# Longformer attention and a squared-ReLU MLP: full-width matmuls issued as two halves of 64 weight columns

## The chip, the cores and the metric

The kernel runs on one core of one Trainium2 chip. The metric is the time of one execution on the device in microseconds, the median of several runs. The profile shows TensorE's matmuls (PE), TensorE's weight loads (PEld), VectorE (DVE), ScalarE (ACT), GpSimd (POOL) and SyncE (SP), which here only issues transfers.

## The reference

Attention over 8 batches and 8 heads with 576 tokens of 64 elements. A token sees its neighbours within 32 positions, and 8 global tokens see all and are seen by all. The heads of a token are then put side by side (4,608 tokens of 512 elements) and go through an MLP.

```python
scores = scale * np.matmul(q, k.transpose(0, 1, 3, 2))
mask = np.abs(pos[:, None] - pos[None, :]) <= window
mask = mask | is_global[:, None] | is_global[None, :]
attn = softmax(np.where(mask, scores, -1e9))      # written out in the reference
x = np.matmul(attn, v) -> (batch * seq, heads * head_dim)
h = x @ w_in                                      # 512 -> 2048
g = np.maximum(h, 0.0) ** 2
out = g @ w_out                                   # 2048 -> 512
```

## The kernel before

All products are in fp16 with fp32 sums. Each matmul on TensorE is two instructions: a weight load, which puts the stationary operand into the array, and the matmul, which streams the moving operand past it. The profile writes the used part of the array as rows*columns, for example 128*128, 128*64 or 64*128, and the moving operand as partitions x columns.

**Attention** goes by units `i` of one batch and two heads, 32 in all, each in two halves of 288 tokens. For a half, `sc_mm` (L758) makes the transposed scores of both heads: 64 rows of the array for each head, so that two matmuls (64*128) share the array. ScalarE takes the exponential (`sc_exp`, L767), VectorE multiplies by the mask (`sc_mask`, L777). `pv_mm` (L799) then multiplies by the values and by a block of ones (which gives the sums): each has 64 weight columns, one head in the columns 0 to 63 and the other in 64 to 127, so that two matmuls (128*64) share the array. A half has 12 such matmuls, or 20 in the first batch's first halves. `pv_rec`, `pv_sum` and `pv_mul` (L809, L818, L840) divide and write `xT`; `scatter` (L861, GpSimd) puts in the rows of the global tokens.

**The MLP** goes by ten chunks of tokens, eight of 512 and two of 256. `mm1` (L526) makes blocks of `x @ w_in` with 128*128 weights and 512 or 256 moving columns; ScalarE takes the maximum with zero (L531), VectorE squares (L533). The first chunk's blocks are made by `mm1_half` (L556) in 256 columns, and its second product by `mm2` (L576) in 512. For the other chunks `mm2_fast` calls `product` (L639), which makes the second product from seven half-size products with 256 moving columns instead of eight; VectorE makes the sums of operands (L612, L618) and of results (L650, L653).

**Preparation.** The first two batches' q and k are transposed on TensorE (`transpose`, L480), with a one-hot product for the global tokens (L485, 8 moving columns). `mask_globals_matmul` (L353) and `values_sum` (L460) use the one-hot `oh` as weights, 8 columns wide. Later batches are transposed by DMA. `warm` (L293) issues matmuls on zeros while TensorE would be idle. `sc_mm` adds the mask by a matmul with the identity (L751) for the early units.

**Order.** The schedule is written out by hand; each engine takes its instructions in program order. MLP pieces wait in the list `fills`, and `fill(n)` takes pieces worth `n` from it between the steps of the attention. In the steady part, units 8 to 31, the order on TensorE is: scores of both halves, MLP pieces, PV of both halves, MLP pieces:

```python
        scores(i, 0)
        scores(i, 1)
        ...
        fill(4)
        ...
        pv_mm(i, 0)
        pv_mm(i, 1)
        ...
        fill(4)
```

So TensorE comes in and out of the scores once per unit, and in and out of the PV matmuls once per unit. After the last unit `take(len(fills))` makes what is left of the MLP.

Of the kernel before, what the change touches and what calls it, by code (L numbers as in the profile page):

```python
# [9 lines left out]
FP16 = mybir.dt.float16  # L10
# [8 lines left out]
NT = 5  # L19
# [3 lines left out]
TP = 96  # L23
# [27 lines left out]
def kernel(  # L51
# [10 lines left out]
    nc = tc.nc  # L62
    B, H, S, D = q.shape
    NG = global_idx.shape[0]
    dm = H * D
    dff = moe_w_in.shape[1]
    P = 128
# [14 lines left out]
    def sbt(name, shape, dtype, bufs=1, tag=None):  # L82
        return sb.tile(shape, dtype, name=name, tag=(tag or name), bufs=bufs)
# [12 lines left out]
    def pst(tag, shape, dtype=FP32):  # L96
        return psum["pool"].tile(shape, dtype, name=tag, tag=tag, bufs=psum["bufs"][tag])
# [12 lines left out]
    def token_rows(nm, i):  # L110
# [11 lines left out]
        for t in (  # L122
# [6 lines left out]
    vts = [  # L129
        early[:, 2 * NT * dm + VW * i : 2 * NT * dm + VW * (i + 1)].rearrange(  # L130
            "p (t e d) -> p t e d", t=NT, e=2
        )
        for i in range(2 * NHP)
    ]
# [88 lines left out]
    idle = sbt("idle", [P, 512], FP16)  # L223
# [18 lines left out]
    for base, cu, cm in (  # L242
# [3 lines left out]
            out=ub[0], in_=ub[0], compare_op=ALU.is_ge, fill=0.0,  # L246
# [4 lines left out]
    for col, base, cm in ((slice(0, 2), -8, 1), (slice(1, 2), KN[-1] + 7, -1)):  # L251
        nc.gpsimd.affine_select(
            out=rows[:, col], in_=rows[:, col], compare_op=ALU.is_ge, fill=0.0,
# [3 lines left out]
        out=ub[1], in_=ub[0], compare_op=ALU.is_ge, fill=0.0,  # L257
# [9 lines left out]
        out=tok, in_=tok, compare_op=ALU.is_ge, fill=-1.0,  # L267
# [7 lines left out]
    identity = sbt("identity", [P, P], FP16)  # L275
# [12 lines left out]
        fetch_tokens(nc.gpsimd, "q", i)  # L288


    def warm(bank, n):
        for _ in range(n):
            nc.tensor.matmul(bank, idle[:, 0:P], idle, start=True, stop=True)  # L293

    def keep_warm(n):
        warm(pst("at", [P, 2, 512])[:, 0], n)

    gbf = sbt("gbf", [P, NG], FP32)
    oh = sbt("oh", [P, NT, NG], FP16)
    ohp = sbt("ohp", [P, TJ, NG], FP16)  # L300

    g16 = sbt("g16", [1, NG], FP16)
# [9 lines left out]
    def one_hots(gb):  # L312
        nc.vector.tensor_copy(out=gbf, in_=gb)
        nc.vector.tensor_tensor(
            out=oh, in0=gbf.unsqueeze(1).to_broadcast((P, NT, NG)),
            in1=tok.unsqueeze(2).to_broadcast((P, NT, NG)), op=ALU.is_equal,
        )
        nc.vector.tensor_tensor(
            out=ohp, in0=gbf.unsqueeze(1).to_broadcast((P, TJ, NG)),
            in1=tokp.unsqueeze(2).to_broadcast((P, TJ, NG)), op=ALU.is_equal,  # L320
        )
# [23 lines left out]
    def mask_globals_matmul():  # L345


        mg = pst("at", [P, 2, 512])
        for half in range(2):
            wins = [x for x in WIN[half] if x[3] > 8]  # L350
            for i, (t, so, c0, w) in enumerate(wins):
                o = c0 - half * BANKC
                nc.tensor.matmul(  # L353
                    mg[0:NG, half, o : o + w], oh[:, t, :],
                    mask[:, MB[half] + so : MB[half] + so + w],
                    start=(i == 0), stop=(i == len(wins) - 1), skip_group_check=True,
                )
        return mg
# [96 lines left out]
    gls = {}  # L455

    def values_sum(i):
        gls[i] = pst("mm", [P, 512])[0:NG, 0 : 2 * D]
        for t in range(NT):
            nc.tensor.matmul(  # L460
                gls[i], oh[:, t, :], vts[i][:, t], start=(t == 0), stop=(t == NT - 1)
            )

    def values_place(i, op):
# [9 lines left out]
    def transpose(nm, i, idles=0):  # L474

        nat = nats[(nm, i)]
        tr = pst("mm", [P, 1024], FP16)
        warm(tr.bitcast(FP32), idles)
        for j in range(TJ):
            nc.tensor.transpose(  # L480
                tr[:, TP * j : TP * j + TP], nat[:, j, :], identity[0:TP, 0:TP]
            )
        gl = tr.bitcast(FP32)[:, 384 : 384 + NG]
        for j in range(TJ):
            nc.tensor.matmul(  # L485
                gl, nat[:, j, :], ohp[0:TP, j, :], start=(j == 0), stop=(j == TJ - 1),
                skip_group_check=True,
            )
        trs[(nm, i)] = tr[:, 0:S].rearrange("p (j q) -> p q j", j=TJ), gl
# [28 lines left out]
    def mm1(c, x):  # L518
        t0, T = CHUNKS[c]
        if c not in gts:  # L520
            gts[c] = sbt("gt", [P, NFF, TC], FP16)
        us = (x, x + NFF // 2) if T < TC else (x // 2 + x % 2 * (NFF // 2),)
        ph = pst("mm", [P, 512]).rearrange("p (j x) -> p j x", x=T)
        for j, u in enumerate(us):
            for t in range(NDM):
                nc.tensor.matmul(  # L526
                    ph[:, j], w_in[:, t, u * P : (u + 1) * P], xT[:, t, t0 : t0 + T],
                    start=(t == 0 and j == 0), stop=(t == NDM - 1), skip_group_check=True,
                )
        rl = sbt("rl", [P, TC], FP16, bufs=5).rearrange("p (j x) -> p j x", x=T)  # L530
        nc.scalar.activation(out=rl, in_=ph, func=AF.Relu)  # L531
        gt = gts[c].rearrange("p (j f) x -> p f j x", j=2)[:, x] if T < TC else gts[c][:, us[0] : us[0] + 1]
        nc.vector.tensor_tensor(out=gt[:, :, 0:T], in0=rl, in1=rl, op=ALU.mult)  # L533
        for p, lo, hi in sums_at(c, x):
            g_sum(c, p, lo, hi)
# [11 lines left out]
    def mm1_half(u, half, tiles=range(NDM)):  # L547

        if 0 not in gts:
            gts[0] = sbt("gt", [P, NFF, TC], FP16)  # L550
        if 0 in tiles:
            ph_now[u] = pst("mm", [P, 2, 256])
        ph = ph_now[u]
        for j in range(2):
            for t in tiles:
                nc.tensor.matmul(  # L556
                    ph[:, j], w_in[:, t, (u + j) * P : (u + j + 1) * P],
                    (xT if half else xA)[:, t, half * 256 : half * 256 + 256],
                    start=(t == 0 and j == 0), stop=(t == NDM - 1), skip_group_check=True,
                )  # L560
        if NDM - 1 not in tiles:
            return
        rl = sbt("rl", [P, TC], FP16, bufs=5).rearrange("p (j x) -> p j x", j=2)
        nc.scalar.activation(out=rl, in_=ph, func=AF.Relu)
        nc.vector.tensor_tensor(
            out=gts[0][:, u : u + 2, half * 256 : half * 256 + 256], in0=rl, in1=rl, op=ALU.mult
        )
# [3 lines left out]
    def mm2(c, m, part):  # L571
        if part == 0:
            po_now[m] = pst("mm", [P, 512])
        po = po_now[m]
        for f in range(part * 4, part * 4 + 4):
            nc.tensor.matmul(  # L576
                po, gts[c][:, f, m * P : (m + 1) * P], w_out[:, f, :],
                start=(f == 0), stop=(f == NFF - 1),
            )
        if part == 3:  # L580
            ot = sbt("ot", [P, dm], FP32, bufs=3)
            nc.vector.tensor_copy(out=ot, in_=po)  # L582
            r0 = CHUNKS[c][0] + m * P
            nc.sync.dma_start(out=out[r0 : r0 + P, :], in_=ot)
# [37 lines left out]
    def product(c, p, bank, s, first=True):  # L622
        if bank not in banks:
            banks[bank] = pst("mm", [P, 2, MH])
        for f in range(FH):
            if p in gsums:
                g = gsums[p][:, f, s * P : (s + 1) * P]
            elif p == 3:
                g = gts[c][:, f, s * P : (s + 1) * P]
            else:  # L630
                r0 = CHUNKS[c][1] // 2 + s * P
                g = gts[c][:, FH + f, r0 : r0 + P]
            if p in wsum:
                w = wsum[p][:, f]
            elif p == 2:
                w = w_out[:, f, 0:MH]
            else:
                w = w_out[:, FH + f, MH:dm]
            nc.tensor.matmul(  # L639
                banks[bank][:, s], g, w, start=(first and f == 0 and s == 0), stop=(f == FH - 1),  # L640
                skip_group_check=True,
            )
# [100 lines left out]
    def sc_mm(i, half, idles=0):  # L743

        kt, qt = kts[i % NBUF], qts[i % NBUF]
        win, W = windows(i, half)
        sc = scs[(i, half)] = pst("at", [P, 2, 512])
        warm(sc[:, 0], idles)
        if added(i, half):
            for e in range(2):  # L750
                nc.tensor.matmul(  # L751
                    sc[:, e, 0:W], identity, far[:, MB[half] : MB[half] + W],
                    start=True, stop=False, skip_group_check=True,
                )
        for t, so, c0, w in win:
            for e in range(2):
                r = slice(64 * e, 64 * e + 64)
                nc.tensor.matmul(  # L758
                    sc[:, e, so : so + w], kt[r, t, :], qt[r, c0 : c0 + w],
                    start=not added(i, half), stop=True, skip_group_check=True,  # L760
                )
# [355 lines left out]
```

## Time and profile before

| | us |
|---|---|
| median of 5 runs | 334.19 (331.57 to 335.84) |
| the profiled execution | 334.61 |
| its span, first to last instruction | 332.9 |
| TensorE matmuls, busy | 316.4 (95%), 3,121 instructions |
| TensorE weight loads, busy | 209.8 (63%), 3,121 instructions |
| VectorE, busy | 244.8 (74%) |
| ScalarE, busy | 202.7 (61%) |
| GpSimd, busy | 127.4 (38%) |

The mean granted clock of TensorE over the span is 0.989: 1.00 but for two stretches of 3.4 us before 36 us, and the last 1 us. A group line gives line, engine, operation, tiles written and read, shape and count; then the busy time of all of them together in us, with overlaps counted once, the mean duration of one in ns, and the engine's idle time just before them with what ended it. Matmuls overlap, so that mean x count is more than the busy time, and the distance between starts is the better measure of what one costs. In the timeline the first column is the start, the second the time from the first start to the last end of the instructions merged in that line.

### The profile page before, as it was taken

Reading aid. Unit: us, or ns where it says so; the run is one execution under the profiler, and the core shown is the slowest. Engines: PE = TensorE matmul, PEld = TensorE weight load, DVE = VectorE, ACT = ScalarE, POOL = GpSimd, SP = SyncE. Lnnn points to the kernel's source line nnn. Section 1 sums busy time; section 2 is a strip of 40 time slices with the busy share of each in tenths; the row PEclk is TensorE's granted clock in tenths of the full one; section 3 lists DMA queues with packets and bytes.
Section 4 is the critical chain, followed back from the end, with each engine's and each line's share of the span. In section 5 each row is a group of like instructions: output and inputs, shape, how many; then the busy total and the mean of one; then the engine's idle time right before and its main releaser. Section 6 shows DMA issues by size and latency. Waiting matters only on the chain.

```text
span 332.9 us, 8222 instructions
## 1 busy us (share of the span) xinstructions
PE 316.4 (95%) x3121; PEld 209.8 (63%) x3121; DVE 244.8 (74%) x600; ACT 202.7 (61%) x380; POOL 127.4 (38%) x222
## 2 busy tenths in 40 slices
PE   7857899999999999999999899999999999999995
PEld 3545677544467647754788645874587458747884
DVE  6746379648997788677867769876987698758465
ACT  3665548654865686668557288658765876363150
POOL 8555786528901960189000962039302000100000
PEclk9997899999999999999999999999999999999999
DMA  8999999999992999399915599369987400200211
GB/s 186 164 186 205 178 193 166 154 109 154 169 121 67 162 178 108 78 175 144 131 66 106 51 175 153 32 143 164 143 64 134 116 2 14 83 32 2 78 50 63
DMA packets 149906, 39.11 MB, mean 117 GB/s; under 512 B 133124, under 2 KB 149300, under 8 KB 149868
## 3 DMA queue, kind: packets, MB, share of 16 engines
q0 software_dynamic: 95408, 16.78, 65.7%
q1 hardware_dynamic: 54042, 21.23, 33.9%
q10 hardware_dynamic: 418, 0.59, 0.7%
q8 instruction: 24, 0.39, 0.5%
q14 instruction: 14, 0.11, 0.1%
HBM read 37.86 MB, written 17.29 MB: 166 GB/s over the span
## 4 chain that ended last, share of the span: by engine, by line
PE 57%; issue 18%; DVE 8%; ACT 5%; POOL 1%; POOLq 0%; DVEq 0%
PE mm L526 23%; PE mm L639 19%; PE at L799 5%; PE mm L556 3%; PE mm L576 3%; PE at L758 3%; ACT er L767 2%; DVE gt L533 2%; DVE mix L618 2%; DVE early L612 1%; DVE xT L840 1%; POOL xT L861 1%; PE mm L480 1%; DVE ot L582 1%; ACT rec L810 1%
## 5 line engine op out<-in xcount | busy, mean ns | idle before, releaser
L526 PE MATMUL mm<-xT,w_in 128*128 128x512 f16 (+1 forms) x576 | 114.3, 356 | 0.1
L531 ACT ACTIVATE rl<-mm 128x512 f16<-128x512 f32 x128 | 75.8, 599 | 36.7 <-PE mm L526 33.5
L526 PEld LDWEIGHTS <-w_in 128*128 128x128 f16 x576 | 55.1, 98 | 52.4 <-issue 0.3
L861 POOL COPY xT<-gx 128x4 f16 x64 | 17.6, 274 | 138.2 <-DVE xT L840 134.8
L533 DVE TENSOR_TENSOR gt<-rl 128x512 f16<-128x512 f16 x128 | 53.2, 423 | 22.5 <-ACT rl L531 20.7
L639 PEld LDWEIGHTS <-mix 128*128 128x128 f16 x640 | 60.7, 98 | 11.0 <-DVE mix L618 1.9
L767 ACT ACTIVATE er<-at 128x880 f16<-128x880 f32 x54 | 46.1, 904 | 15.3 <-PE at L758 15.3
L618 DVE TENSOR_TENSOR mix<-gt 128x1024 f16<-128x1024 f16 (+1 forms) x82 | 53.2, 673 | 0.2
L639 PE MATMUL mm<-early,mix 128*128 128x256 f16 x384 | 45.6, 273 | 1.2 <-DVE mix L618 1.2
L777 DVE TENSOR_TENSOR et<-er,mask 128x880 f16<-128x880 f16 x54 | 33.3, 617 | 17.5 <-ACT er L767 16.9
L809 ACT ACTIVATE rec<-at 128x288 f32<-128x288 f32 x64 | 25.8, 404 | 32.2 <-PE at L799 27.1
L840 DVE TENSOR_TENSOR xT<-at,rec 128x288 f16<-128x288 f32 x60 | 27.2, 453 | 9.7 <-ACT rec L810 9.0
L639 PE MATMUL mm<-early,gt 128*128 128x256 f16 x256 | 31.9, 273 | 0.7 <-DVE gt L533 0.4
L639 PE MATMUL mm<-w_out,mix 128*128 128x256 f16 x256 | 30.6, 273 | 0.0
L799 PE MATMUL at<-et,onesb 128*64 128x192 f16 (+5 forms) x400 | 30.3, 228 | 0.0
L810 ACT ACTIVATE rec<-rec 128x288 f32<-128x288 f32 x64 | 28.4, 443 | 2.0
L653 DVE TENSOR_TENSOR ot<-mm,pt 128x512 f32<-128x512 f32 (+1 forms) x36 | 22.7, 632 | 8.0 <-ACT pt L678 6.8
L639 PEld LDWEIGHTS <-gt 128*128 128x128 f16 x256 | 23.9, 98 | 6.9 <-DVE gt L533 2.0
L178 POOL DMA_DIRECT2D kscr<-in_k_dram x30 | 26.2, 1065 | 2.4 <-DMA w_out<-in_moe_w_out_dram 2.1
L185 POOL DMA_DIRECT2D qscr<-in_q_dram x24 | 23.8, 1400 | 0.6 <-DMA gscr_k<-gstk 0.6
L799 PEld LDWEIGHTS <-onesb 128*64 128x64 f16 x400 | 22.2, 113 | 0.0
L678 ACT COPY pt<-mm 128x512 f32<-128x512 f32 (+1 forms) x18 | 9.7, 539 | 20.4 <-PE mm L639 20.4
(121 smaller groups left out, 348.6 us busy)
## 6 DMA issues: line engine op xcount, KB each, us to landing
out_dram<-ot SPq DMA_DIRECT2D x32, 256.0 KB
qscr<-in_q_dram POOLq DMA_DIRECT2D x24, 144.0 KB, 7.7
kscr<-in_k_dram POOLq DMA_DIRECT2D x24, 120.0 KB, 4.1
w_in<-in_moe_w_in_dram POOLq DMA_DIRECT2D x4, 512.0 KB, 7.1
w_out<-in_moe_w_out_dram POOLq DMA_DIRECT2D x4, 512.0 KB, 16.8
stf<-in_v_dram POOLq DMA_DIRECT2D x12, 120.0 KB, 6.0
s16b<-in_v_dram POOLq DMA_DIRECT2D x12, 120.0 KB, 8.3
early<-in_v_dram SPq DMA_DIRECT2D x20, 60.0 KB
```

Source lines behind the costliest of these rows:

```text
L178: nc.gpsimd.dma_start(out=kscr[b][r0 : r0 + KN[t]].rearrange("s (h d) -> s h d", d=D), in_=k[b, :, KT * t : KT * t + KN[t]].rearrange("h s ...
L526: nc.tensor.matmul(ph[:, j], w_in[:, t, u * P : (u + 1) * P], xT[:, t, t0 : t0 + T], start=(t == 0 and j == 0), stop=(t == NDM - 1), skip_ ...
L531: nc.scalar.activation(out=rl, in_=ph, func=AF.Relu)
L533: nc.vector.tensor_tensor(out=gt[:, :, 0:T], in0=rl, in1=rl, op=ALU.mult)
L618: nc.vector.tensor_tensor(out=gsums[p][:, lo:hi, 0:TH], in0=g[0], in1=g[1], op=op)
L639: nc.tensor.matmul(banks[bank][:, s], g, w, start=(first and f == 0 and s == 0), stop=(f == FH - 1), skip_group_check=True,)
L767: nc.scalar.activation(out=er[:, :, 0:W], in_=scs.pop((i, half))[:, :, 0:W], func=AF.Exp, bias=0.0, scale=scale)
L777: nc.vector.tensor_tensor(out=et[:, :, 0:W], in0=er[:, :, 0:W], in1=mask[:, MB[half] : MB[half] + W].unsqueeze(1).to_broadcast((P, 2, W)), ...
L799: nc.tensor.matmul(acc[D * e : D * e + D, x, o : o + w], onesb if x else vt[:, t, e], et[:, e, so : so + w], start=(n == 0), stop=(n == le ...
L809: nc.scalar.activation(out=rec, in_=av[:, 1, :, 0:GTOK], func=AF.Ln)
L810: nc.scalar.activation(out=rec, in_=rec, func=AF.Exp, scale=-1.0)
L840: nc.vector.tensor_tensor(out=(xT if x0 else xA)[:, hp, x0 : x0 + HS].rearrange("p (k x) -> p k x", k=2), in0=av[:, 0, :, 0:GTOK], in1=rec ...
```

## The change

Every matmul that used all 128 weight columns is issued as two: weight columns 0 to 63 to the output's partitions 0 to 63, then columns 64 to 127 to partitions 64 to 127, both with the same moving operand. A new helper `halves` does it for `warm`, the one-hot product in `transpose`, `mm1`, `mm1_half`, `mm2`, `product` and the identity product in `sc_mm`; the transposes proper get their own loop. The one-hot `oh` is widened from 8 to 64 columns, cleared once, so that its two users have 64 weight columns as well. The PV matmuls had 64 columns already and stay. The scores keep 64*128, and the one small product of `indices` keeps its shape. Sums, sizes of buffers, and the order of the pieces stay as they were.

```diff
+    def halves(to, weights, moving, **flags):
+        for r in (slice(0, P // 2), slice(P // 2, P)):
+            nc.tensor.matmul(to[r], weights[:, r], moving, **flags)
+
     def warm(bank, n):
         for _ in range(n):
-            nc.tensor.matmul(bank, idle[:, 0:P], idle, start=True, stop=True)
+            halves(bank, idle[:, 0:P], idle, start=True, stop=True)
...
-    oh = sbt("oh", [P, NT, NG], FP16)
+    oh = sbt("oh", [P, NT, D], FP16)
+    nc.vector.memset(oh, 0.0)
...
-            out=oh, in0=gbf.unsqueeze(1).to_broadcast((P, NT, NG)),
+            out=oh[:, :, 0:NG], in0=gbf.unsqueeze(1).to_broadcast((P, NT, NG)),
...
-                    mg[0:NG, half, o : o + w], oh[:, t, :],
+                    mg[0:D, half, o : o + w], oh[:, t, :],
...
-        gls[i] = pst("mm", [P, 512])[0:NG, 0 : 2 * D]
+        gl = pst("mm", [P, 512])[0:D, 0 : 2 * D]
+        gls[i] = gl[0:NG]
         for t in range(NT):
             nc.tensor.matmul(
-                gls[i], oh[:, t, :], vts[i][:, t], start=(t == 0), stop=(t == NT - 1)
+                gl, oh[:, t, :], vts[i][:, t], start=(t == 0), stop=(t == NT - 1)
             )
...
         for j in range(TJ):
-            nc.tensor.transpose(
-                tr[:, TP * j : TP * j + TP], nat[:, j, :], identity[0:TP, 0:TP]
-            )
+            for r in (slice(0, D), slice(D, P)):
+                nc.tensor.transpose(
+                    tr[r, TP * j : TP * j + TP], nat[:, j, r], identity[0:TP, 0:TP]
+                )
         gl = tr.bitcast(FP32)[:, 384 : 384 + NG]
         for j in range(TJ):
-            nc.tensor.matmul(
+            halves(
                 gl, nat[:, j, :], ohp[0:TP, j, :], start=(j == 0), stop=(j == TJ - 1),
...
             for t in range(NDM):
-                nc.tensor.matmul(
+                halves(
                     ph[:, j], w_in[:, t, u * P : (u + 1) * P], xT[:, t, t0 : t0 + T],
...
         for f in range(part * 4, part * 4 + 4):
-            nc.tensor.matmul(
+            halves(
                 po, gts[c][:, f, m * P : (m + 1) * P], w_out[:, f, :],
...
-            nc.tensor.matmul(
+            halves(
                 banks[bank][:, s], g, w, start=(first and f == 0 and s == 0), stop=(f == FH - 1),
...
             for e in range(2):
-                nc.tensor.matmul(
+                halves(
                     sc[:, e, 0:W], identity, far[:, MB[half] : MB[half] + W],
```

The same replacement in `mm1_half` is left out here.

More of the change, by code (lines that the diff above doesn't have):

```diff
@@ L750, in sc_mm @@
             for e in range(2):
-                nc.tensor.matmul(
+                halves(
                     sc[:, e, 0:W], identity, far[:, MB[half] : MB[half] + W],
```

## The prediction

> **What bounds the kernel now.** I began with the busy table and the slices, then the chain of work that ended last, then the costliest groups, and last the timeline of TensorE.
>
> ```profile
> PE 316.4 (95%) x3121; PEld 209.8 (63%) x3121; DVE 244.8 (74%) x600; ACT 202.7 (61%) x380; POOL 127.4 (38%) x222
> ...
> PE 57%; issue 18%; DVE 8%; ACT 5%; POOL 1%; POOLq 0%; DVEq 0%
> ...
> L526 PE MATMUL mm<-xT,w_in 128*128 128x512 f16 (+1 forms) x576 | 114.3, 356 | 0.1
> ...
> L639 PE MATMUL mm<-early,mix 128*128 128x256 f16 x384 | 45.6, 273 | 1.2 <-DVE mix L618 1.2
> ```
>
> TensorE is busy 95% of the span, and its matmuls lead the chain. The two MLP lines waited 0.1 us and 1.2 us. By stretches PE is busy 30.4 of the first 40 us, 66.3 of 40 to 107, 190.9 of 107 to 300, and 28.7 of the last 32.9. So from 40 to 300 us time on TensorE is time of the kernel; before 40 us PE often waits for others, and after 300 us no attention is left.
>
> A busy PE can still lose time between matmuls. The timeline of TensorE shows it (start, duration, line, tiles, array rows*columns, shape, count):
>
> ```profile
> 221.65 2.46 PE L639 MATMUL mm<-early,mix 128*128 128x256 f16 x21
> 224.03 0.26 PE L799 MATMUL at<-et,stf 128*64 128x160 f16 x2
> 224.13 0.23 PE L799 MATMUL at<-et,onesb 128*64 128x160 f16 x2
> 224.20 0.25 PE L799 MATMUL at<-et,stf 128*64 128x192 f16 x2
> 224.28 0.25 PE L799 MATMUL at<-et,onesb 128*64 128x192 f16 x2
> 224.36 0.21 PE L799 MATMUL at<-et,stf 128*64 128x88 f16 x2
> 224.40 0.21 PE L799 MATMUL at<-et,onesb 128*64 128x88 f16 x2
> 224.44 0.22 PE L799 MATMUL at<-et,stf 128*64 128x112 f16 x2
> ...
> 224.76 0.23 PE L799 MATMUL at<-et,onesb 128*64 128x136 f16 x2
> 224.92 3.41 PE L526 MATMUL mm<-xT,w_in 128*128 128x512 f16 x15
> ```
>
> The 21 full-width matmuls of 256 columns last 2.46 us, one of them 0.273 us, so they start every (2.46-0.273)/20 = 109 ns. Those of 512 start every (3.41-0.38)/14 = 216 ns. The difference gives 0.418 ns per moving column and some 2 ns beside it. The last of the first group started at 221.65+2.46-0.273 = 223.84 and had streamed by 223.94; the first PV matmul starts at 224.03, about 95 ns later. The last PV pair, at 224.76, had streamed its 136 columns by 224.82; the next full-width matmul starts at 224.92, some 100 ns later. Neither gap has a releaser: it is the price of changing the way the array is divided. Scores (64*128) pay the same, 98 ns in and 95 ns out.
>
> **Part 1, the gaps that go.** I went through the matmuls in order of their starts. Full width and 128*64 are neighbours at 66 places, each some 97 ns (92 to 125, one of 244). From 40 to 300 us there are 60, together 5.87 us. After the change full width is 128*64, so these gaps shrink to the usual 2.5 ns: 5.87 - 60x0.0025 = 5.72 us. The second start after a change is late too: 94 ns after the first of 160 columns where 69 is usual (25 ns, some 28 times), 227 where 216 is usual (11 ns, some 32 times): 1.05 us more. Around the scores nothing goes: from 128*64 into the scores costs 98 ns and back 92, the few times that before has them, against 98 and 95 from full width. But coming out of the scores the second start is then late by 25 ns, not 11: 30 x 14 ns = 0.42 us to pay. Counted over the program, neighbours of different division fall from 154 to 80.
>
> **Part 2, a pair in the place of one matmul.** This is the dangerous part: 1,894 matmuls become pairs, 1,664 of them (576 of L526, 896 of L639, 128 of L556, 64 of L576) in the MLP. The PV rows above are such pairs: "x2" is two halves whose records start 2 to 4 ns apart. Pairs of 192 columns follow each other in 80 to 85 ns, of 88 in 40; over all PV the medians are 83, 60, 49.5 and 39 ns for 192, 136, 112 and 88 columns, where 0.418 ns per column and 2.5 would be 82.7, 59.3, 49.3 and 39.3. A pair therefore costs what one matmul does, to within some 0.35 ns. 1,664 x 0.35 = 0.6 us to pay. Below nothing I see no room: the columns must stream.
>
> [...] The rows:
>
> ```profile
> L526 PEld LDWEIGHTS <-w_in 128*128 128x128 f16 x576 | 55.1, 98 | 52.4 <-issue 0.3
> ...
> L799 PEld LDWEIGHTS <-onesb 128*64 128x64 f16 x400 | 22.2, 113 | 0.0
> ```
>
> A half load does last longer, 113 ns against 98. But 400 of them fill only 22.2 us, so they overlap, and pairs of 88 columns follow in 40 ns with two loads each. Loads of the two halves run beside each other and are no limit at 109 ns. [...]
>
> **Part 3, the small things.** In 16 transposes, 96 one-hot products of 8 columns go from 25 ns to the 30 ns of an 8-column PV pair; half of them lie after 40 us: 0.25 us. [...] Half rows in the accumulators change nothing for ScalarE and VectorE, which still wait for the second half. No DMA moves.
>
> **The sum.** 5.72 + 1.05 - 0.42 - 0.6 - 0.25 = 5.5 us on TensorE between 40 and 300 us. Beside gaps of this kind PE idles there some 7 us in spots where VectorE is later (0.5 us before the scores at 221 and 254 us, 1.2 us at 189); there a faster PE only waits longer, so I pass on 93%: 5.1 us. With the early 0.1 either way: 334.61 us of the profiled execution (span 332.9 and 1.7 around it) become 329.5. That execution stands 0.4 above the median of 334.19, so the median forecast is 329.1.
>
> **Rival 1: it does what it says and the gain is lost on the way.** A pair that costs 2 ns more than one matmul takes 3.3 us back, and VectorE (148 of 193 us busy from 107 to 300) or the half-speed clock that the early waits bring (0.50 granted in two stretches of 3.4 us, at 24.9 and 31.7) another 1 us: 333 to 334. For it: no pair longer than 192 columns is in the trace, and in none do both halves read the same moving data, as all will. Against: the four widths lie on one line. Chance 0.18.
>
> **Rival 2, on the other side: the front end.** PE's instructions grow from 6,244 to 10,032 in the program. A 256-column step, today two instructions in 109 ns, becomes four: 27 ns each. [...] The PV burst (48 instructions in 0.75 us) doesn't refute it, since the engine's queue could have been filled ahead. What speaks against it is PE's own semaphore steps, seen for the PV line while PE was still in the MLP:
>
> ```profile
> L799 PEldq EVENT_SEMAPHORE  x3: 51/51/51, 190.1 to 190.3; - x3
> ```
>
> They stand 125 ns apart, and the program has 8 instructions (4 MATMULs) between one and the next; less the 51 ns step that is 9 ns each, 31 ns a MATMUL at most with everything counted. Where the queue was full (222.0 to 222.9) the same steps stand 436 ns apart, the pace of the array. Instruction fetch grows from 24 to some 40 blocks of 16 KB, each 0.9 to 2.0 us and needed every 7 us. Chance 0.10, and 0.05 for a pair that costs over 5 ns more for another reason (both halves on the same addresses): 338 to 342.
>
> **How the numbers follow.** Forecast 0.67, 329.1 with 326.5 to 331.5 (pair cost 0 to 1 ns, share passed on 0.8 to 1.1, the early clock 1.5 us either way). Rival 1, 331.5 to 336. Slower cases 0.15, from 337 up. About 0.04 lie under 326.5 and 0.15 above 336, so the range is 326.5 to 336. One per cent is what a measurement can tell from no change (330.9 and 337.5 are its ends): faster 0.67, same 0.19, slower 0.14.
>
> **What would show it.** Right: in the timeline of after, a 256-column pair every 109 to 110 ns and a 512-column pair every 216; the PV pair following the MLP pair with no 95 ns; 98 and 92 ns still at the scores. Wrong: pairs at 113 ns and more, or pairs whose second half starts a full stream after the first; "issue" gaps between pairs in long MLP runs; a granted clock under 1.00 after 40 us.

## The result, and the profile after

The changed kernel takes 332.23 us (median of 42 runs, 329.68 to 336.46) against 333.46 us (79 runs): a ratio of 0.9971, 95% interval 0.9957 to 0.9984. By that ratio it is 1.0 us faster where 5.1 us were forecast. The ratio, here and below, is that of the runs in the faster of each kernel's two states, so it isn't quite that of the medians. The time lies in the range; the gain is a fifth of the one predicted. The profiled execution of the changed kernel took 335.48 us (span 333.7), 3.2 us above its own median, so the two profiled totals are not compared below; stretches of the two traces are.

The page of the changed kernel: its busy table, its instruction queue (transfers, MB) and its costliest groups (busy us, mean ns | idle before):

```profile
PE 313.3 (94%) x5015; PEld 239.5 (72%) x5015; DVE 244.9 (73%) x601; ACT 202.1 (61%) x380; POOL 127.3 (38%) x222
...
q8 instruction: 39, 0.64, 0.8%
...
L293 PE MATMUL mm<-xT,w_in 128*64 128x512 f16 (+1 forms) x1280 | 124.0, 350 | 2.3 <-DVE ot L589 2.0
L293 PEld LDWEIGHTS <-w_in 128*64 128x64 f16 x1408 | 80.8, 110 | 46.8 <-issue 6.7
...
L293 PE MATMUL mm<-early,mix 128*64 128x256 f16 x768 | 45.8, 273 | 1.2 <-DVE mix L625 1.2
```

All the full-width matmuls now stand at line 293, the helper. Twice the number of matmuls of 256 columns keep TensorE busy for 45.8 us, against 45.6 before: the pairs run side by side. A half load lasts 110 ns against 98, and it hides. What is new is at the end of the first L293 row: TensorE waited 2.0 us for `ot` of VectorE, which it did not do before. And the instruction queue brought 39 blocks of 16 KB in the place of 24 (`q8 instruction: 24, 0.39, 0.5%` on the page of before).

The timeline of TensorE in the changed kernel around a block of scores, where before had 95 to 100 ns on either side of the PV matmuls:

```profile
220.28 0.23 PE L806 MATMUL at<-et,s16b 128*64 128x136 f16 x2
220.34 0.23 PE L806 MATMUL at<-et,onesb 128*64 128x136 f16 x2
220.40 1.91 PE L293 MATMUL mm<-early,mix 128*64 128x256 f16 x32
222.25 0.36 PE L765 MATMUL at<-qt,kt 64*128 64x160 f16 x6
223.07 0.37 PE L765 MATMUL at<-qt,kt 64*128 64x112 f16 x6 [0.46 <-DVE xT L847]
223.37 2.81 PE L293 MATMUL mm<-early,mix 128*64 128x256 f16 x48
```

The last PV pair starts at 220.34 and streams 136 columns, 0.06 us; the MLP starts at 220.40. That gap is gone. The 32 halves in 1.91 us are 16 pairs every (1.91 - 0.273)/15 = 109 ns. So the pairs cost what the forecast said, and the gaps go where it said. But two lines below stands the other half of the story: in the middle of the scores TensorE waits 0.46 us for VectorE, and that wait has grown. The same place in before:

```profile
221.01 0.37 PE L758 MATMUL at<-qt,kt 64*128 64x112 f16 x6 [0.35 <-DVE xT L840]
```

**The steady part, counted.** Between the same two score blocks (starts at 101.28 and 280.33 us before, 104.43 and 281.22 after) I took, for each matmul, its start less the end of the stream of the one before. Gaps of 60 to 140 ns, the price of a change of division, fell from 8.08 to 3.94 us: 4.1 us, as forecast for the 44 places there (4.2 us). Longer gaps, each of which VectorE ends, rose from 8 with 3.44 us to 13 with 5.47. The stretch itself went from 179.05 to 176.79 us: 2.3 us of 4.1, or 55%, came through. It isn't the noise of one profile: in all eleven traces with `mm1` and `product` halved this stretch takes 175.95 to 176.79 us, and in the five with both at full width 179.03 to 179.15; so 2.3 to 3.1 us of 4.2 come through. TensorE's waits from 100 to 285 us, before and then after (us in total, times, longest):

```profile
PE mm L639 <- DVE mix L618: 1.0, 1, 1.0
PE at L758 <- DVE xT L840: 0.7, 2, 0.3
```

```profile
PE mm L293 <- DVE gt L540: 1.1, 2, 0.7
PE mm L293 <- DVE mix L625: 1.0, 1, 1.0
PE at L765 <- DVE xT L847: 0.9, 2, 0.5
PE at L806 <- DVE et L784: 0.2, 1, 0.2
```

VectorE sets TensorE's start at more places, and at the old ones a little later.

**The early part, lost twice.** At 44 us the changed kernel's scores stood 1.8 us ahead of before's (42.63 against 44.45). At 61 us the lead was 0.2 us, at 83 us it had become a delay of 2.9 us (86.08 against 83.15). The first loss has no semaphore in it. Two parts of TensorE's timeline after, from 43 to 54 us:

```profile
43.84 0.33 PE L487 MATMUL mm<-identity,natk 96*64 96x96 f16 x4
44.46 0.32 PE L487 MATMUL mm<-identity,natk 96*64 96x96 f16 x5 [0.29 <-issue]
45.23 0.26 PE L487 MATMUL mm<-identity,natk 96*64 96x96 f16 x3 [0.45 <-issue]
...
52.13 0.17 PE L293 MATMUL mm<-ohp,natq 96*64 96x8 f16 x1
52.91 0.33 PE L293 MATMUL mm<-ohp,natq 96*64 96x8 f16 x11 [0.61 <-issue]
53.09 1.04 PE L293 MATMUL mm<-xT,w_in 128*64 128x256 f16 x16
```

Twelve transposes that belong together are torn into 4, 5 and 3; a group of twelve gathers into 1 and 11. "issue" says that the engine waited for nothing that the profile shows. The second loss has a releaser, here in the timelines of TensorE and of VectorE:

```profile
78.73 3.64 PE L293 MATMUL mm<-xT,w_in 128*64 128x512 f16 x32
84.39 1.76 PE L293 MATMUL mm<-xT,w_in 128*64 128x512 f16 x8 [2.01 <-DVE ot L589]
```

```profile
83.64 0.69 DVE L589 COPY ot<-mm 128x512 f32<-128x512 f32 x1 [2.84 <-DMA out_dram<-ot]
```

Before ran five accumulators through at the same place, with no wait:

```profile
78.73 4.48 PE L526 MATMUL mm<-xT,w_in 128*128 128x512 f16 x20
```

An accumulator here is a block of sums that takes one bank, a buffer of the pool `pst` in the memory called PSUM; eight half matmuls or four full ones fill it. In the changed kernel the fifth after the first chunk waits for its bank; the fourth output copy frees it; the copy needs one of three `ot` buffers, and waits 2.84 us until the first output has landed. TensorE stood still for 2.0 us, and its clock was granted at half for the next 3.4 us (from 84.6 us).

### The profile page after: what moved, and what is told of

Its sections match the earlier page's. It is cut to its first block, busy times and chain, and to the rows that moved or that the text cites. A ratio compares the mean times of both kernels' runs of the same rounds, so it can differ in the third digit from the quotient of the medians.

```text
span 333.7 us, 12010 instructions
## 1 busy us (share of the span) xinstructions
PE 313.3 (94%) x5015; PEld 239.5 (72%) x5015; DVE 244.9 (73%) x601; ACT 202.1 (61%) x380; POOL 127.3 (38%) x222
## 4 chain that ended last, share of the span: by engine, by line
issue 44%; POOL 21%; DMA 20%; PE 11%; POOLq 1%; DVE 1%; SPq 0%; ACT 0%
PE mm L293 11%; DMA qscr<-in_q_dram 5%; DMA w_out<-in_moe_w_out_dram 5%; POOL kscr L178 5%; DMA early<-in_v_dram 4%; POOL qscr L185 4%; POOL xT L868 4%; DMA qt<-qscr 3%; POOL s16b L207 2%; POOL stf L207 2%; DMA w_in<-in_moe_w_in_dram 2%; DMA stf<-in_v_dram 1%; POOL mix L868 1%; POOLq L868 1%; POOL s16b L152 1%
## 5 line engine op out<-in xcount | busy, mean ns | idle before, releaser
L293 PE MATMUL mm<-xT,w_in 128*64 128x512 f16 (+1 forms) x1280 | 124.0, 350 | 2.3 <-DVE ot L589 2.0
L293 PEld LDWEIGHTS <-w_in 128*64 128x64 f16 x1408 | 80.8, 110 | 46.8 <-issue 6.7
L538 ACT ACTIVATE rl<-mm 128x512 f16<-128x512 f32 x128 | 74.8, 599 | 39.9 <-PE mm L293 37.0
L293 PEld LDWEIGHTS <-mix 128*64 128x64 f16 x1280 | 68.5, 110 | 3.5 <-DVE mix L625 1.7
L293 PE MATMUL mm<-early,mix 128*64 128x256 f16 x768 | 45.8, 273 | 1.2 <-DVE mix L625 1.2
L816 ACT ACTIVATE rec<-at 128x288 f32<-128x288 f32 x64 | 25.8, 404 | 26.3 <-PE at L806 22.9
L293 PEld LDWEIGHTS <-gt 128*64 128x64 f16 x640 | 34.5, 110 | 8.7 <-DVE gt L540 2.4
L293 PE MATMUL mm<-early,gt 128*64 128x256 f16 x512 | 32.0, 273 | 1.5 <-DVE gt L540 1.4
L293 PE MATMUL mm<-w_out,mix 128*64 128x256 f16 x512 | 30.9, 273 | 0.0
L765 PEld LDWEIGHTS <-kt 64*128 64x128 f16 x400 | 12.6, 97 | 15.3 <-issue 13.6
```

Source lines behind the costliest of these rows:

```text
L293: nc.tensor.matmul(to[r], weights[:, r], moving, **flags)
```

## The experiments

Every ratio is to the kernel before, timed beside it. The theory at the start: the main part (mm1 and the weight product) gains, and something takes the gain away; the first question was where.

### Twice the same, and the two parts alone

> The kernel before, a second profile of it. Theory F (floor): until about 73 us the transfers and GpSimd set when unit 8 may start; the start of the MLP's main part does not depend on TensorE, so unit 8's scores start at 72 to 74 us again. Theory C (clock): half-width matmuls wake TensorE's clock later than full-width ones; then the clock of before reaches 1.00 at about 8 us again, as in its first profile (7.8 us).

> The changed kernel, a second profile of it. Theory F: unit 8's scores start at 72 to 74 us whatever the early clock does, and from there to the end each unit is 0.2 us shorter than before. [...]

Before again took 333.91 us, after again 333.99, one run each. Neither theory held. Unit 8's scores began at 72.2 and 73.3 us, as F had said, but at 69.4 in `e1_main` below, so there is no such floor; and C, by which the halved kernel gets its full clock late (16.3 us in its first profile), fell with the 6.9 us of `a2`. Single profiles of one kernel can stand 5 us apart at 30 us already: the seventh block of scores begins at 30.3 us in `a_bank` and at 25.1 in `a_again`, the same kernel further down. The early clock is granted differently in each, in full from 6.6 to 18.7 us on and then at half for stretches of 3.4 to 13.7 us. Both losses were there again in `a2`: three pauses (0.64, 0.51 and 0.77 us) from 44 to 55 us, and 1.63 us of waiting on `ot` at 84 us.

`e1_main` is before with halves in two places only; `e2_early` has them everywhere else:

```
-                nc.tensor.matmul(
+                halves(
                     ph[:, j], w_in[:, t, u * P : (u + 1) * P], xT[:, t, t0 : t0 + T],
...
-            nc.tensor.matmul(
+            halves(
                 banks[bank][:, s], g, w, start=(first and f == 0 and s == 0), stop=(f == FH - 1),
```

> Halves only in mm1 and product, the main part of the MLP; everything before and chunk 0's MLP stay full width. Theory F: the 0.2 us per unit of the steady part stays whole, so 3 to 4.5 us less than before and as fast as the changed kernel or up to 1.5 us faster: 329.5 to 332. Theory C: the gain that the changed kernel loses early comes back, 328.5 to 330. If the main part itself takes something back, 332.5 or more.

> The complement: halves in everything but mm1 and product. Theory F: no change within 0.7 us of before (332.8 to 334.2), since what is gained before 73 us waits for transfers. Theory C: slower than before by 1.5 to 3 us, 335 to 336.5. The sum of the changes of e1_main and e2_early should be the change of the whole, -1.2 us, within 1 us.

`e1_main` took 332.07 us, ratio 0.9976 (0.9952 to 0.9999); `e2_early` 335.55 us, 1.0058 (1.0030 to 1.0085). The early edits alone make the kernel slower; the time lies where C had put it, although C had fallen. The changes of the two parts, -0.8 and +1.9 us, do not add up to the whole, -1.0; they had been expected to, within 1 us. In both traces TensorE stood still near 80 us until the fourth output copy had ended (1.18 us, which the profile puts down to "issue" although the copy ended 0.06 us earlier, and 1.11 us), so that wait comes with either part, and neither part's halves can be its cause by themselves.

### The banks

In the compiled programs the `mm` accumulators are the same tiles in the same order in both kernels, but not in the same PSUM banks. Which bank is given out is decided when the program is built. From the fifth accumulator after the first chunk on, the plan of the changed kernel differs (bank 3 where that of before took bank 1); so does that of the 13 accumulators of the preparation, from the fourth on. I wrote the order of before into the changed kernel by hand, and the reverse:

```
+    BANK = {3: iter("0100100101010"), 2: iter("0321032103201320...")}
...
+        if tag == "mm":
+            tag = "mm" + next(BANK[psum["bufs"]["at"]])
+            return psum["pool"].tile(shape, dtype, name="mm", tag=tag, bufs=1)
```

> The changed kernel with each accumulator of the MLP placed by hand in the bank that it had in the kernel before. Theory B (bank): the wait of TensorE at about 84 us comes from the other bank, and goes: 1 to 2 us less than the changed kernel, 330 to 331.2, and no wait of over 0.3 us between unit 8's PV and unit 9's scores. Theory F (transfers set the floor): the wait only moves to the next scores, time as the changed kernel's, 331.8 to 332.8.

> The kernel before, full width, with the accumulators placed by hand in the banks that the changed kernel uses. Theory B: it gets the wait at about 80 to 84 us, 0.8 to 1.8 us slower than before: 333.8 to 335. Theory F: as before within 0.4 us.

> Halves in mm1 and product alone, with the banks of the kernel before. Theory B: the steady gain of 2.5 us or so comes through whole: 330 to 331. Theory F: as without the banks, about 332.

> Halves in everything but mm1 and product, with the banks of the kernel before. Theory B: of the 2 us that this kernel lost to the kernel before, 1 us comes back: 333.8 to 334.8; what is left (0.5 to 1.5 us) is the early part's own loss, in transposes and the clock. Theory F: 335.5 again. If the early part alone gains as its gaps promise, it is below 333.

The changed kernel with the banks of before took 331.76 us, ratio 0.9943 (0.9916 to 0.9969); before with the banks of the changed one 334.57 us, 1.0031 (1.0008 to 1.0055). `e1_bank`, `e1_main` with the banks of before, took 331.26 us, 0.9917 (0.9894 to 0.9941), and `e2_bank` 334.66 us, 1.0027 (1.0002 to 1.0051). All four move the same way, by 0.3 to 0.6%: 1.0 to 2.0 us for a choice that no line of the diff makes. The time of `a_bank` missed its forecast (330 to 331.2), and that of `e1_bank` missed by 0.3 us.

The traces are the firmer evidence. The thirteenth block of scores begins at 61 us in before and the seventeenth at 83. This stretch takes 21.4 to 22.2 us in all ten traces with the banks of before, and 22.9 to 25.2 in all six with those of the changed kernel, whatever is halved. And `b_bank`, full width everywhere, has the wait at the fifth accumulator:

```profile
77.62 3.62 PE L531 MATMUL mm<-xT,w_in 128*128 128x512 f16 x16
82.46 1.02 PE L531 MATMUL mm<-xT,w_in 128*128 128x512 f16 x4 [1.22 <-DVE ot L587]
```

With the banks of before it goes from this place, but where everything is halved a part comes back one accumulator later, just after the scores: 0.45 us in `a_bank`, 0.87 in `a_again`.

The main part's halves bring 2.8 us (0.9917), and the early edits still cost 0.9 us (1.0027) with the banks as they were.

### The pauses

Looked at instruction by instruction, TensorE stops in the early part before instructions that carry no wait. A pause is given here as the distance between two starts; the idle time in the rows is less. Counted from 0 over its weight loads, matmuls and semaphore instructions in order of their starts, it stopped before number 1729 in the changed kernel, in `a2`, `a_bank` and `e2_bank`, before 705 in the changed kernel and `a_bank`, and before 1985 in the changed kernel and `e2_bank`. These numbers are multiples of 256 apart, and the transfers of 16 KB on the instruction queue agree: the changed kernel has 3,788 loads and matmuls more and 15 such transfers more, 253 for each. I call the numbers the grid. At each of them the pause ended 2.2 to 2.5 us after such a transfer had started (for 1729 in the changed kernel: start 50.53, landed 51.41, next instruction 52.91). Before has no such pause between 40 and 62 us. From the eighth to the thirteenth block of scores (44 to 61 us in before) the four traces with everything halved take 18.0 to 18.4 us, the seven with `mm1_half` at full width 16.1 to 16.6.

The grid does not explain all of it. The transposes torn into 4, 5 and 3 above lie off it (numbers 1358 and 1368), and those two pauses, 0.49 and 0.64 us, are nearly half of the 2.4 us in that trace.

Three experiments: the transposes and their gathers alone back to full width (`e3_tr`, the other halves and the banks of before kept); the reverse, `e1_bank` with only these halved (`e4_dense`); and `e1_bank` with a run of small matmuls at its end, to see the supply by itself (`m_fetch`).

```
-            for r in (slice(0, D), slice(D, P)):
-                nc.tensor.transpose(
-                    tr[r, TP * j : TP * j + TP], nat[:, j, r], identity[0:TP, 0:TP]
-                )
+            nc.tensor.transpose(
+                tr[:, TP * j : TP * j + TP], nat[:, j, :], identity[0:TP, 0:TP]
+            )
...
-            halves(
+            nc.tensor.matmul(
                 gl, nat[:, j, :], ohp[0:TP, j, :], start=(j == 0), stop=(j == TJ - 1),
```

```
     take(len(fills))
+    tail = pst("at", [P, 2, 512])[:, 0, 0:8]
+    for _ in range(400):
+        nc.tensor.matmul(tail, idle[:, 0:P], idle[:, 0:8], start=True, stop=True)
+    for _ in range(400):
+        halves(tail, idle[:, 0:P], idle[:, 0:8], start=True, stop=True)
```

> The changed kernel with the accumulator banks of before, and only the transposes with their gathers (48 instructions a pair of tiles) put back to full width. Instruction supply theory: the early part loses because the halved transposes use up instructions at 90 in a us, and TensorE then pauses with no semaphore wait (0.6 to 1.1 us each, at instruction 1344, 1729 and 1985 of TensorE in the profiles) until the next 16 KB of its program is there. At full width the pauses go (about 2.0 us), and eight changes of width near four groups of transposes come back (8 x 97 ns = 0.8 us): 1.2 us less than with the halves, ratio about 0.991, no pause over 0.4 us without a wait between 40 and 62 us. Rival, that the early part loses to the clock or to the first transfers: the pauses stay or move, only the changes of width are added, ratio about 0.997.

> The kernel with halves in mm1 and the product alone and the banks of before (ratio 0.9917), and the transposes with their gathers halved as well; mm1_half and mm2 stay full. Supply theory: pauses without a wait come into the early part, where the transposes follow full-width matmuls at 18 instructions in a us, so fewer than in the changed kernel: 0.5 to 1.5 us, and eight changes of width add 0.8 us; ratio 0.996 to 0.999. Rival (clock or transfers): no pauses, 0.8 us of changes alone, ratio 0.994.

> The best kernel so far, with 400 full-width matmuls of 8 columns and then 400 pairs of halves of 8 columns at its end, which nothing waits for; they are extra work and no part of the computation. Supply theory: 800 instructions at 80 in a us (10 us) meet three pauses of about 1 us, 1600 at 130 in a us (12 us) meet six of about 1.5 us, one in every 256 instructions, each ending about 2.4 us after the start of a 16 KB instruction transfer; the whole about 34 us, though the transfers of data are over by then. Rival (pauses come from full data queues only, or from the first part alone): no pauses, 22 us.

`e3_tr` took 329.04 us, 0.9866 (0.9817 to 0.9915), and no pause was left between 40 and 62 us. `e4_dense` took 329.50 us, 0.9904 (0.9869 to 0.9939), against 0.9917 for `e1_bank`: halving the transposes cost nothing there, and its trace has no pause either. I had expected 0.5 to 1.5 us of pauses; with 0.9904 both theories missed (0.996 to 0.999, and 0.994). One measure accounts for both runs: the time from the start of a transfer to the first instruction of the block that it brings (on the grid: 1217, 1473, 1729, 1985). For transfers between 40 and 62 us it is 6.7 and 10.4 us in before, 5.4 and 6.7 in `e3_tr` and 3.2 and 3.7 in `e4_dense`. Wherever TensorE paused on the grid it is 2.2 to 2.5 us, and in no trace is it anywhere shorter than 2.2. The transfers of this part start some 75 to 265 instructions ahead of their block. With everything halved, the two transposes of a pair of tiles and their gathers are 96 instructions in some 0.9 us, and `mm1_half` four in 109 ns: a hundred instructions can pass in 1.0 us. Full-width transposes are 48 in the same 0.9 us, and halved ones beside a full-width `mm1_half` (two in 109 ns) are followed by a slower stretch. In both the block is there in time. What starts a transfer is not shown by the traces.

`m_fetch` took 361.02 us. Its tail lasted 33.2 us, near the 34 expected, but not for the reason given. The timeline of TensorE at its end:

```profile
348.29 3.58 PE L298 MATMUL at<-idle 128*64 128x8 f16 x128
352.02 6.13 PE L298 MATMUL at<-idle 128*64 128x8 f16 x213 [0.15 <-issue]
```

The whole groups between pauses are 128 matmuls, that is 256 instructions with their loads. The longest steps stand before numbers 10177, 10433, 10689, 10945, 11201 and 11457, each 256 after the last and on the same grid as 1729; they end 2.3 to 2.6 us after the start of a transfer, in the quiet end of the program. So the period and the delay were right, and full data queues are not needed for them. But the steps last 0.17 and 0.34 to 0.35 us, two of them only 0.07 where 0.05 is usual, not 1.5; and the full-width run had none (2.7 and 2.8 us from transfer to block): here the transfer began 145 to 210 instructions ahead, and 75 passed in a us, less than the 130 that I had put in. Most of the length of the tail goes with the clock, which was granted at half from 329.3 us to the end: the pairs of 8 columns stood 53 ns apart there, where the PV pairs of 8 columns took 30 at the full clock.

### Are the two losses separate?

`e5_tr_only` is the changed kernel with the same lines of `transpose` back to full width, and the scheduler's own choice of banks (that of the changed kernel from the fifth accumulator on).

> The changed kernel with only the transposes and their gathers put back to full width; the scheduler chooses the banks, and from the fifth accumulator after the first chunk on its choice is that of the changed kernel, not that of before. If the pauses of the instruction supply and the banks are two separate losses, this run keeps the second and is free of the first: the ratio of the changed kernel, 0.9971, less what the transposes brought with the banks of before (0.9943 to 0.9866, -0.0077): 0.989, no pause without a wait over 0.4 us between 40 and 62 us, and TensorE's wait of 1 to 2 us on VectorE near 80 us. Rival, that e3's gain was the clock or a lucky set of runs: 0.994 to 0.998, as with the halved transposes.

331.37 us, 0.9951 (0.9930 to 0.9973): the 0.989 of the theory is outside, and the rival's 0.994 to 0.998 came true, though not its reason, as the next pair shows. The pauses at 52 and 59 us were gone, but one of 0.52 us stayed at 44.8, and TensorE stood still for 1.32 us at 82 us until the output copy had ended. So with the banks of the changed kernel, full-width transposes bring 0.20% (0.9971 to 0.9951), where with those of before they had brought 0.77%. The pair was run once more side by side:

> The kernel of e3_tr once more (banks of before, transposes at full width, all else halved), now beside its pair with halved transposes on one chip. Width of the transposes and banks as two separate losses: full-width transposes bring what they brought with the changed kernel's banks, 0.9971 to 0.9951, so 0.9923 here against 0.9943. The one hiding the other (the wait of TensorE on VectorE near 80 us takes what the early part gains, and with the banks of before nothing takes it): 0.986 to 0.989, as in the five runs of e3_tr.

> The kernel of a_bank once more (banks of before, everything halved), as the other half of the pair: 0.9943 by its earlier runs, whichever holds; the difference to e3_again is the price of halving the transposes where the wait near 80 us is out of the way: 0.2% if the losses are separate, 0.5 to 0.8% if that wait hid it.

`e3_again` took 328.92 us, 0.9854 (0.9832 to 0.9876); `a_again` 330.39 us, 0.9897 (0.9865 to 0.9929). Both came out lower than forecast. `a_again` is the kernel of `a_bank`, whose ratio on another chip was 0.9943: so a difference of under 0.5% between kernels timed apart decides little here. The difference of the pair, 0.43% or 1.4 us, lies between the two expectations, and its intervals do not decide. What is firm is the corner: from the changed kernel to `e3_again` the two edits together bring 0.9971 to 0.9854, 3.9 us, and the share of each depends on which is made first (0.7 and 3.2 us with the transposes first; 0.9 to 2.5 and then 1.4 or more with the banks first). They are not separate. The likely reason, not tested by itself, is that the wait near 80 us takes part of whatever TensorE gains ahead of it; some of it is left even in `a_again` (0.87 us), none in `e3_again`.

The timeline of TensorE in `a_again`, only the rows that "issue" released:

```profile
43.83 0.38 PE L298 MATMUL mm<-xT,w_in 128*64 128x256 f16 x3 [0.43 <-issue]
...
50.29 0.33 PE L298 MATMUL mm<-ohp,natq 96*64 96x8 f16 x11 [0.80 <-issue]
...
57.31 0.20 PE L298 MATMUL mm<-ohp,natk 96*64 96x8 f16 x3 [0.83 <-issue]
```

The matmuls that follow the pauses are numbers 1473, 1729 and 1985, 256 apart. The same place in `e3_again`, without a pause:

```profile
48.13 0.43 PE L491 MATMUL mm<-identity,natk 96*128 96x96 f16 x6
48.40 0.30 PE L496 MATMUL mm<-ohp,natk 96*128 96x8 f16 x6
48.55 0.42 PE L491 MATMUL mm<-identity,natq 96*128 96x96 f16 x6
48.80 0.30 PE L496 MATMUL mm<-ohp,natq 96*128 96x8 f16 x6
49.02 1.06 PE L298 MATMUL mm<-xT,w_in 128*64 128x256 f16 x16
50.02 0.36 PE L769 MATMUL at<-qt,kt 64*128 64x112 f16 x6
53.40 0.26 PE L810 MATMUL at<-et,early 128*64 128x160 f16 x2 [3.01 <-DVE xT L851]
```

The last row shows what is late next: TensorE reached this PV 3.0 us too soon. VectorE, which has to release it, was itself held by the transfer of some values (its timeline in `e3_again`):

```profile
50.71 0.43 DVE L463 CAST early<-early 128x512 f16<-128x512 f32 x1 [3.00 <-DMA early<-in_v_dram]
```

All the runs with an interval together (H is halved, F full width):

| kernel | mm1, product | mm1_half, mm2 | transposes | banks of | us | ratio |
|---|---|---|---|---|---|---|
| before | F | F | F | before | 333.5 | 1 |
| b_bank | F | F | F | after | 334.57 | 1.0031 |
| e1_main | H | F | F | after | 332.07 | 0.9976 |
| e1_bank | H | F | F | before | 331.26 | 0.9917 |
| e4_dense | H | F | H | before | 329.50 | 0.9904 |
| e2_early | F | H | H | after | 335.55 | 1.0058 |
| e2_bank | F | H | H | before | 334.66 | 1.0027 |
| after | H | H | H | after | 332.23 | 0.9971 |
| a_bank, a_again | H | H | H | before | 331.76, 330.39 | 0.9943, 0.9897 |
| e5_tr_only | H | H | F | after | 331.37 | 0.9951 |
| e3_tr, e3_again | H | H | F | before | 329.04, 328.92 | 0.9866, 0.9854 |

The best version is the last: 1.5% faster than before, 1.2% faster than the change.

## Why the prediction was wrong

Its mechanism was right, and its end was not: a gain of 1.0 us in the place of 5.1.

- **Part 1, the gaps that go: right.** 4.1 us of them went in the steady part, where the forecast's price gives 4.2 for its 44 places, and PV follows the MLP without a gap. Out of and into the scores 92 and 98 ns stayed, as said.
- **Part 2, the pair: right.** 109 ns for 256 columns, 216 for 512. Rival 1's pair of 2 ns more does not exist, and the weight loads of 110 ns hide, as the rows had said.
- **The sum, "so I pass on 93%": this step failed.** In the steady part 55% came through, and 75% in the best trace. I took the idle time beside VectorE as a stock that would stay what it was; the share of 93% had no working, and its "some 7 us" are 5.3 us at 15 places when counted as above. But a place at which VectorE releases TensorE can swallow the gain collected since the last such place, and their number grew from 8 to 13, their time by 2.0 us. With 55% of the 5.5 us the forecast would have been near 3 from this step alone.
- **The sum again: two terms were missing.** It had no price for the supply of instructions: of 2.4 us of pauses from 44 to 60 us in the profile of after, 0.78 and 0.45 us lie on the grid of 256; the other two, 0.49 and 0.64, lie off it, and their cause stays open, though all four were gone in `e3_tr`. Rival 2 had the right resource and the wrong measure. It noted 16 KB blocks "needed every 7 us" against 0.9 to 2.0 us each; that is the mean over the run. At the transposes a hundred instructions pass in some 1.0 us, and a block takes 2.2 to 2.5 us from the start of its transfer to its first instruction. Nor does TensorE run short inside long MLP runs: pairs of 256 columns, four instructions each, hold 109 ns. No run shows a term for the slower cases, from 337 us up: the median of the changed kernel is 332.23 us, and that of `e2_early`, the slowest of all the runs with an interval, 335.55.
- **Nor had it a price for the banks.** I had written that the sizes of the buffers and the order of the work stay, and inferred that nothing moves but widths. Which bank an accumulator gets is decided anew at each build; here it put the fifth accumulator after the first chunk behind an output copy that waits for a transfer: 2.0 us at 84 us, 1.1 to 1.6 us in five other traces with these banks.
- **Part 3** put the transposes at 0.25 us, by their own length. Their length was right; what cost was that they double the instructions at the densest place of the program, and only together with a halved `mm1_half`: beside a full-width one they cost nothing (`e4_dense`, 0.9904 against the 0.9917 of `e1_bank`). No run shows the early 0.1 us of the sum: in the profile of after the clearing of `oh` took 0.19 us, and the first mask product began at 5.60 us, against 5.67 before.

With the two missing terms undone the kernel is at 328.9 us, next to the forecast of 329.1. That the two meet is partly luck: 1.0 us of the 4.1 is lost in the steady part even there (`e3_tr`: 175.96 us for the stretch that took before 179.05), and by subtraction the early part must bring the rest, some 1.5 us; I have not followed where.

## What to carry to other kernels

Cost a doubled instruction count at the densest hundred or two hundred instructions of the program, not by the mean: here TensorE ran dry where the rest of a block passed within some 2.4 us of the start of the next transfer, and putting the 24 small matmuls per pair of tiles back to full width was enough to stop it on the grid. When a kernel's tile pools choose their buffers at build time, compare the chosen places of both builds, since a new choice can cost as much as the edit brings (here 1.0 to 2.0 us, against 1.0). And pass a gain on only as far as the next place where another engine releases the first one: count those places.

## What the hardware showed beyond that

- TensorE's program arrived in blocks of 256 instructions (the pauses of `a_again` stand before numbers 1473, 1729 and 1985), and a pause for it looks like "issue" in the profile (0.43, 0.80 and 0.83 us there), with no releaser. The delay at a pause (2.2 to 2.6 us from the start of the transfer) was much the same in the busiest transfers of the early part and in the quiet end of `m_fetch`.
- Not settled: some early pauses lie off the grid (numbers 1341 to 1386 in five of the traces, in pairs of 0.35 to 0.67 us that let eight to ten instructions through between them, while a transfer is just beginning; the 0.52 us of `e5_tr_only`). I have only seen that they too come without a wait and beside halved early work or its transposes.
- In `m_fetch` TensorE lost its clock while it issued without a break: matmuls of 8 columns, every 25 ns, began at 325.2 us; the granted clock fell to half at 329.3 and stayed there for the remaining 32 us of records.
- The first full clock comes at 6.6 to 10 us in some runs and at 16 to 19 us in others (7.8 before, 16.3 after, 6.9 in `a2`, 16.5 in the full-width `b_bank`). It follows neither the width nor the number of instructions. It sets profiles some 3 us apart at the third block of scores (16.0 us in before, 18.9 in `b_bank`), but by the seventh that can be gone (29.0 and 28.2).
